# A gated recurrence and a low-rank mixer on one core: every operation in another order, the unread products placed anew

## The chip, the core and the metric

The kernel runs on one core of a Trainium2 chip. The core's engines work side by side, each through its own queue in the order in which the program issued to it: TensorE (PE in the profile, with PEld for its weight loads), VectorE (DVE), ScalarE (ACT), GpSimd (POOL) and SyncE (SP), which here issues nearly all DMA transfers. An instruction that needs another engine's result waits on a semaphore, and everything behind it in its queue waits with it. The metric is device time in microseconds (us), lower is better; the median of the kernel before is 626.9 us over 3 runs (626.64 to 627.37).

## What is computed

Two blocks in a row. The first is a recurrence over 768 steps for 4 batches, 8 heads of width 48; the second takes its output as a matrix of 4 x 768 x 384 and applies a rank-32 mixing along the sequence and a two-layer product along the channels:

```python
mag = np.sqrt(a_re * a_re + a_im * a_im)
scale = np.minimum(mag, 0.999) / (mag + 1e-06)
a_re_n, a_im_n = (a_re * scale, a_im * scale)
for t in range(S):
    new_re = ar * S_re - ai * S_im
    new_im = ar * S_im + ai * S_re
    S_re, S_im = (new_re + kv, new_im)
    y[:, :, t] = np.einsum('bhd,bhde->bhe', q[:, :, t], S_re)
...
h = xt @ U @ V
u = x + h.transpose(0, 2, 1)
ch = np.maximum(u @ w_ch1, 0.0) @ w_ch2
return (u + ch)
```

All inputs reach the kernel as float32 except the weights U, V, w_ch1 and w_ch2, whose 64-bit words the kernel converts itself.

## The kernel before

**Tiling.** The sequence is cut into 24 chunks of 128 steps (4 batches of 6), and two chunks make a group, so there are 12 groups. For each group, `gates` turns a_re and a_im into decays: ACT and DVE compute log magnitudes (tile GL, or GS as two halves), PE sums them within a chunk (tiles `es ps`, `ef ps`, and `tot` for blocks), ACT takes exponentials (es, ef, E), and SP moves E into T. The angles go the same way through `ph`, F and the sines in cs. `prep` multiplies q and k by these (DVE, tile qk and then QKC), and PE turns the result (tile `tr`), which ACT copies to QK. `chain` is then PE's own part of a chunk: `inner`, `corners`, `dk` and `y`, with DVE and ACT work between them. `mixer` runs over two chunks at a time, and only once a batch's 6 chunks are there: `rank`, `mixed`, `uTp`, then the large products `up` or `few` (w_ch1) and `down` (w_ch2). The weights are converted piece by piece on DVE and ACT in between (tags w1 and w2, tile stage).

**Order.** None of these functions issues anything. Each calls `plan.add` with an engine, a tag such as ("gates", 4) and a function that will issue the instructions. There are 2671 such operations. The table ORDER at the head of the file gives each its place, a number from 0 to 2670, under its engine and tag, and `Plan.order` sorts by it. The order on each engine's queue, and on SP's, is the order of these places; it also fixes the order in which buffers are handed out. The operations, their sizes and their costs do not depend on it.

**Unread products.** A second table, SPARE, maps a place to a number of units. Before the operation at that place, the program calls `idle` until those units are used up, at most 3 units (AHEAD) at a time. `idle(k)` issues one PE product of the 128 x 128 identity with k times 128 columns, into a PSUM tile that some later operation will overwrite from the start; nobody reads it. It finds no tile when every such tile is in use, and then issues nothing and the units are gone.

```python
            out += [-1] * SPARE.get(at[n], 0) + [n]
...
        while run:
            idle(min(run, AHEAD))
            run -= min(run, AHEAD)
```

Each 32-bit PE product leaves two MATMUL records in the trace, so 3 units are two records of 128 x 384. In the file before, these products are at L1519; the change shortens the file by one line, so that every line of the kernel stands one lower there (L1518).

Of the kernel before, what the change touches and what calls it, by code (L numbers as in the profile page):

```python
# [39 lines left out]
        ("POOL", "load"): {0: [14], 1: [34], 1.5: [84], 2: [31]},  # L40
        ("DVE", "load"): {1: [58]},
# [6 lines left out]
        ("ACT", "gates"): {0: [1, 2, 4, 6, 7, 16, 17, 22, 23, 29, 28, 45, 70, 71], 1: [24, 27, 38, 39, 41, 42, 46, 47, 65, 64, 67, 68], 2: [129, 108,  # L48
# [10 lines left out]
        ("DVE", "gates"): {0: [5, 8, 13, 18, 19, 54, 49], 1: [30, 21, 40, 43, 44, 51, 50], 2: [111, 143, 156, 185, 169], 4: [277, 322, 323, 372, 356],  # L59
# [10 lines left out]
        ("ACT", "angles"): {0: [72, 86, 98, 100, 103], 1: [76, 106, 112, 114, 126], 2: [210, 231, 251, 240, 241, 242, 263, 269, 271], 4: [375, 395,  # L70
# [5 lines left out]
        ("DVE", "angles"): {0: [81, 89], 1: [87, 107], 2: [211, 232, 252], 4: [376, 402, 425], 6: [589, 597, 602, 612, 625, 626, 665], 8: [698, 716,  # L76
# [4 lines left out]
        ("DVE", "prep"): {0: [85, 104, 110], 1: [121, 128, 145], 2: [226, 250, 265], 3: [203, 304, 309], 4: [373, 424, 427], 5: [443, 470, 472], 6:  # L81
# [99 lines left out]
class Plan:  # L181
# [33 lines left out]
    def order(self):  # L215
# [9 lines left out]
        for n in sorted(range(len(at)), key=lambda n: at[n]):  # L225
# [9 lines left out]
            done.add(n)  # L235
            out += [-1] * SPARE.get(at[n], 0) + [n]
        return out
# [1351 lines left out]
```

## Time and profile before

| | |
|---|---|
| median of 3 runs | 626.9 us |
| the profiled execution's own span | 627.0 us |
| PE busy with products | 609.9 us (97%) |
| PE busy with weight loads | 526.2 us (84%) |
| DVE busy | 499.7 us (80%) |
| ACT busy | 415.8 us (66%) |
| POOL busy | 38.1 us (6%) |
| DMA | 45.74 MB, mean 73 GB/s |

How to read it: a busy share is the part of the span in which an engine had work under way. It is an average over stages. The records of matmuls carry modelled ends, so that one product's end can lie after the next one's start; where a cost is wanted, the distance from one start to the next is the safer number. A timeline row gives start, duration, engine, line, operation and tiles, then how many records it merges, and in brackets how long the engine had been idle before and what it was waiting for. A row of the windows view gives, for a stretch of the span, how long each engine was busy in it, the clock that was granted to PE as a share of full speed, and the DMA share and rate.

### The profile page before, as it was taken

Reading aid. Unit: us, or ns where it says so; the run is one execution under the profiler, and the core shown is the slowest. Engines: PE = TensorE matmul, PEld = TensorE weight load, DVE = VectorE, ACT = ScalarE, POOL = GpSimd, SP = SyncE. Lnnn points to the kernel's source line nnn. Section 1 sums busy time; section 2 is a strip of 40 time slices with the busy share of each in tenths; the row PEclk is TensorE's granted clock in tenths of the full one; section 3 lists DMA queues with packets and bytes.
Section 4 is the critical chain, followed back from the end, with each engine's and each line's share of the span. In section 5 each row is a group of like instructions: output and inputs, shape, how many; then the busy total and the mean of one; then the engine's idle time right before and its main releaser. Section 6 shows DMA issues by size and latency. Waiting matters only on the chain.

```text
span 627.0 us, 23447 instructions
## 1 busy us (share of the span) xinstructions
PE 609.9 (97%) x10380; PEld 526.2 (84%) x10380; DVE 499.7 (80%) x887; ACT 415.8 (66%) x807; POOL 38.1 (6%) x79
## 2 busy tenths in 40 slices
PE   6998989999999999999999999999999999999998
PEld 3566767666889889889989989888999998999997
DVE  6899999888999979758977867788989884464554
ACT  6999999999898988687787867688433431202010
POOL 5000000000001010010000100000100100000100
PEclk7999999999999999999999999999999999999999
DMA  8864565644143252541512512601203020000101
GB/s 211 191 146 115 135 136 132 155 111 104 33 80 76 50 120 44 99 89 28 99 37 46 113 40 46 124 19 25 63 21 60 9 51 3 1 1 1 45 14 44
DMA packets 173685, 45.74 MB, mean 73 GB/s; under 512 B 167632, under 2 KB 170384, under 8 KB 173584
## 3 DMA queue, kind: packets, MB, share of 16 engines
q1 hardware_dynamic: 171376, 39.90, 30.1%
q0 software_dynamic: 2208, 4.35, 2.1%
q8 instruction: 81, 1.33, 0.9%
q14 instruction: 20, 0.16, 0.1%
HBM read 33.59 MB, written 4.72 MB: 61 GB/s over the span
## 4 chain that ended last, share of the span: by engine, by line
PE 77%; ACT 4%; DVE 3%; DMA 1%; issue 1%; SPq 0%; ACTq 0%; DVEq 0%
PE down L1356 24%; PE up L1122 15%; PE few L1222 11%; PE dk L996 3%; PE tr L860 3%; PE y L1035 3%; PE inner L910 2%; PE down L1313 2%; PE inner L907 2%; PE tot L741 2%; PE y L1027 2%; PE mixed L1089 2%; PE es ps L692 1%; PE ef ps L692 1%; PE uTp L1107 1%; PE corners L971 1%
## 5 line engine op out<-in xcount | busy, mean ns | idle before, releaser
L1122 PE MATMUL up<-uT,w 128*128 128x256 f32 x504 | 116.9, 383 | 0.0
L387 DVE TENSOR_TENSOR QK<-QK,T 112x512 f32<-112x512 f32 (+2 forms) x144 | 102.1, 732 | 8.4 <-PE inner L910 4.3
L1122 PEld LDWEIGHTS up<-uT,w 128*128 128x128 f32 x504 | 93.6, 190 | 12.5
L1356 PE MATMUL down<-w,h 128*128 128x192 f32 x396 | 72.2, 331 | 0.0
L384 ACT ACTIVATE gate<-gate 128x768 f32<-128x768 f32 (+1 forms) x82 | 64.8, 795 | 7.4 <-DVE GS L791 3.2
L1356 PEld LDWEIGHTS down<-w,h 128*128 128x128 f32 x396 | 64.1, 190 | 1.5 <-issue 0.7
L871 ACT COPY QK<-tr 112x512 f32<-112x512 f32 x96 | 51.2, 590 | 14.6 <-PE tr L860 14.3
L390 DVE TENSOR_TENSOR xo<-down,xo 128x192 f32<-128x192 f32 (+1 forms) x79 | 29.9, 387 | 27.5 <-PE down L1356 27.0
L387 DVE TENSOR_TENSOR QKC<-qk,cs 128x768 f32<-128x768 f32 x44 | 41.7, 955 | 6.3 <-ACT cs L384 3.6
L1230 ACT COPY h<-few 128x512 f32<-128x512 f32 x30 | 17.2, 586 | 40.8 <-PE few L1222 40.8
L1356 PE MATMUL down<-stage 128*128 128x192 f32 x198 | 37.6, 331 | 0.0
L1111 ACT COPY uT<-uTp 128x384 f32<-128x384 f32 x22 | 10.0, 479 | 41.4 <-PE uTp L1107 26.9
L1222 PE MATMUL few<-gate,w 128*128 128x128 f32 x280 | 34.8, 275 | 0.0
L1298 POOL DMA_DIRECT2D out_dram<-xo x32 | 19.2, 644 | 243.3 <-DVE xo L390 140.0
L860 PEld LDWEIGHTS tr<-ident,QKC 64*112 64x112 f32 x768 | 24.5, 130 | 10.7 <-issue 4.7
L1222 PEld LDWEIGHTS few<-gate,w 128*128 128x128 f32 x280 | 33.3, 192 | 0.0
L1356 PEld LDWEIGHTS down<-stage 128*128 128x128 f32 x198 | 32.1, 190 | 0.7 <-issue 0.2
L779 POOL DMA_DIRECT2D gate<-F x15 | 12.0, 799 | 327.9 <-DVE w L578 113.5
L860 PE MATMUL tr<-ident,QKC 64*112 64x64 f32 x768 | 29.4, 221 | 2.3 <-DVE QKC L387 1.6
L381 ACT ACT_TABLE_LOAD x24 | 30.8, 1283 | 1.1 <-PEq L1573 0.7
L384 ACT ACTIVATE h<-up 128x512 f32<-128x512 f32 x42 | 24.6, 596 | 9.8 <-PE up L1122 9.5
L976 ACT COPY AT<-corners 32x128 f32<-32x128 f32 x96 | 24.2, 255 | 9.6 <-PE corners L971 8.3
(200 smaller groups left out, 1285.4 us busy)
## 6 DMA issues: line engine op xcount, KB each, us to landing
stage<-in_moe_w_ch_dram SPq DMA_DIRECT2D x12, 768.0 KB, 5.0
qk<-in_q_dram SPq DMA_DIRECT2D x24, 192.0 KB, 3.2
qk<-in_k_dram SPq DMA_DIRECT2D x24, 192.0 KB, 2.7
VP<-in_v_dram SPq DMA_DIRECT2D x24, 192.0 KB, 3.6
gate<-in_a_re_dram SPq DMA_DIRECT2D x22, 192.0 KB, 3.4
gate<-in_a_im_dram SPq DMA_DIRECT2D x22, 192.0 KB, 3.4
AT<-DG SPq DMA_DIRECT2D x96, 32.0 KB, 2.3
T<-E SPq DMA_DIRECT2D x48, 48.0 KB, 2.9
```

What stands on the lines that cost most here:

```text
L381: ACT(1.37, rank, lambda: nc.scalar.preload_act_table_set(name), writes=[TABLE])
L384: return nc.scalar.activation(out=o, in_=i, func=f, **kw)
L387: nc.vector.tensor_tensor(out=o, in0=a, in1=b, op=OP.mult)
L390: nc.vector.tensor_tensor(out=o, in0=a, in1=b, op=OP.add)
L860: nc.tensor.transpose(out=get(*ps[r])[0:DQ, h], in_=get(*qkc)[at, h].rearrange("p u d -> p (u d)")[:, 0:DQ], identity=ident[at, at], tile_ ...
L871: nc.scalar.copy(out=to, in_=a)
L976: ACT(0.36, RR, lambda r=r, u=u: nc.scalar.copy(out=get(*ATi).rearrange("p (a u) t -> p a u t", u=2)[r:r + BLK, :, u, BLK:2 * BLK], in_=ge ...
L996: nc.tensor.matmul(out=get(*dk[r])[x:end, h], lhsT=get(*ks)[at, h, x // DP, 0:end - x], rhs=get(*VPi)[at, h], start=True, stop=True, tile_ ...
L1122: nc.tensor.matmul(out=get(*ps)[:, e], lhsT=w1[:, f, (ff + e) * 128:(ff + e + 1) * 128], rhs=get(*uT)[:, f], start=(f == 0), stop=(f == KD ...
L1222: nc.tensor.matmul(out=get(*ps)[:, q], lhsT=w()[:, q * 128:(q + 1) * 128], rhs=v[0](), start=(n == 0 and q == 0), stop=True, skip_group_ch ...
L1298: queue.dma_start(out=out[b, c * CH:(c + 1) * CH, lo:hi], in_=get("xo", i)[:, lo:hi])
L1356: nc.tensor.matmul(out=get(*to)[:, part], lhsT=x(j), rhs=y[:, j], start=(first and j == 0), stop=(j == KH - 1), skip_group_check=not first)
```

## The change

Both tables are replaced and nothing else: the same 2671 operations under the same engines and tags, with the same number under each, get other places, and SPARE asks for unread products at other places. Before, SPARE asked for 153 units at 41 places up to place 718. After, it asks for 229 units at 22 places up to place 619, 60 of them ahead of place 21. As the tables feed the same program, the built queues show what comes of it: before, 46 unread products of together 91 units stand on PE's queue, since `idle` found no tile for the rest; after, 83 products stand there, and they are all of the 229 units.

The first PE operations, `es ps` and `ef ps` of the first chunk, stand behind one product run of 8 units before and of 60 units after. The tables, cut to their beginnings (ORDER is some 140 lines):

```diff
 ORDER = {
-        ("SP", "load"): {0.0: [0, 3, 2666, 2654, 2670], 0.05: [11, 12], 0.1: [9], 1: [10], 1.2: [57], 1.3: [15, 59], 1.4: [83], 2: [35], 2.5: [56,
...
-        ("PE", "gates"): {0: [20, 32, 69], 1: [62, 63, 66], 2: [162, 163, 167, 168, 187, 188], 4: [331, 339, 343, 351, 352, 355], 6: [543, 525, 550,
...
+        ('SP', 'load'): {0.0: [1, 3, 2666, 2663, 2670], 0.05: [15, 6], 0.1: [8], 1: [27], 1.2: [22], 1.3: [73, 36], 1.4: [95], 2: [35], 2.5: [96, 66],
...
+        ('PE', 'gates'): {0: [21, 41, 52], 1: [45, 48, 54], 2: [156, 179, 161, 184, 185, 196], 4: [324, 344, 350, 355, 358, 360], 6: [532, 513, 533,
...
-SPARE = {20: 8, 32: 9, 62: 1, 66: 1, 73: 1, 82: 5, 91: 1, 113: 6, 116: 1, 119: 8, 140: 8, 153: 6, 157: 4, 167: 1, 168: 1, 207: 6, 216: 1, 217: 1, 282:
-         1, 352: 2, 436: 1, 514: 5, 518: 5, 527: 4, 546: 4, 547: 25, 551: 12, 596: 2, 601: 1, 606: 3, 624: 1, 632: 3, 646: 1, 653: 1, 664: 1, 672: 2,
-         678: 5, 694: 1, 695: 1, 717: 1, 718: 2}
+SPARE = {21: 60, 45: 13, 52: 3, 78: 13, 94: 6, 101: 21, 115: 9, 141: 28, 148: 6, 156: 4, 177: 8, 185: 3, 208: 5, 225: 4, 242: 2, 265: 13, 268: 4, 408:
+         9, 474: 4, 479: 3, 491: 6, 619: 5}
```

PE's queue in the order after, up to the first large block: 60 units, `es ps` and `ef ps` of chunk 0, 13 units, `es ps` and `ef ps` of chunk 1, 3 units, `tot`, two `ph` products, 13 units, two more `ph`, 6 units, the third kind of `ph`, 21 units, `tr` twice, 9 units, `dk`, `tr`, `inner`, 28 units. On SP's queue, the load of q for chunk 0 stands behind the first move of E into T; before, it stood ahead of all of them.

More of the change, by code (lines that the diff above doesn't have):

```diff
@@ L30 @@
 ORDER = {
[9 rows of a table removed]
-        ("POOL", "load"): {0: [14], 1: [34], 1.5: [84], 2: [31]},
-        ("DVE", "load"): {1: [58]},
[6 rows of a table removed]
-        ("ACT", "gates"): {0: [1, 2, 4, 6, 7, 16, 17, 22, 23, 29, 28, 45, 70, 71], 1: [24, 27, 38, 39, 41, 42, 46, 47, 65, 64, 67, 68], 2: [129, 108,
[10 rows of a table removed]
-        ("DVE", "gates"): {0: [5, 8, 13, 18, 19, 54, 49], 1: [30, 21, 40, 43, 44, 51, 50], 2: [111, 143, 156, 185, 169], 4: [277, 322, 323, 372, 356],
[10 rows of a table removed]
-        ("ACT", "angles"): {0: [72, 86, 98, 100, 103], 1: [76, 106, 112, 114, 126], 2: [210, 231, 251, 240, 241, 242, 263, 269, 271], 4: [375, 395,
[5 rows of a table removed]
@@ L76 @@
-        ("DVE", "angles"): {0: [81, 89], 1: [87, 107], 2: [211, 232, 252], 4: [376, 402, 425], 6: [589, 597, 602, 612, 625, 626, 665], 8: [698, 716,
[4 rows of a table removed]
-        ("DVE", "prep"): {0: [85, 104, 110], 1: [121, 128, 145], 2: [226, 250, 265], 3: [203, 304, 309], 4: [373, 424, 427], 5: [443, 470, 472], 6:
[6 rows of a table removed]
-        ("ACT", "prep"): {0: [115, 117, 120, 122], 1: [158, 147, 154, 160], 2: [266, 270, 283, 281], 3: [319, 320, 327, 318], 4: [442, 439, 446, 445],
[4 rows of a table removed]
-        ("DVE", "rest"): {0: [118, 149, 155, 175, 159, 170, 194], 1: [174, 229, 234, 259, 209, 235, 248, 253], 2: [288, 315, 325, 366, 291, 314, 324,
[8 rows of a table removed]
@@ L102 @@
-        ("DVE", "levels"): {0: [123, 135, 148, 136, 137, 152], 1: [177, 192, 202, 195, 198, 225], 2: [292, 302, 308, 301, 303, 312], 3: [328, 371,
[9 rows of a table removed]
-        ("ACT", "levels"): {0: [138], 1: [215], 2: [305], 3: [378], 4: [468], 5: [530], 6: [766], 7: [839], 8: [947], 9: [1006], 10: [1152], 11:
[14 rows of a table removed]
-        ("ACT", "rest"): {0: [191, 182, 200, 201, 219, 223, 222], 1: [255, 261, 256, 258, 280, 279, 278], 2: [342, 341, 336, 335, 385, 390, 391], 3:
[10 rows of a table removed]
-        ("ACT", "small"): {0: [595, 285, 307, 492, 396, 554, 590, 549, 623, 636], 1: [744, 791, 777, 807, 782, 856, 859], 2: [984, 978, 1088, 1139,
[4 rows of a table removed]
@@ L143 @@
-        ("DVE", "small"): {0: [246, 600, 631, 637, 640, 638, 685, 682, 603, 607, 731, 737], 1: [705, 741, 690, 817, 843, 844, 870, 871, 889, 913, 912,
[25 rows of a table removed]
-        ("POOL", "small"): {0: [932, 933], 1: [1119, 1116, 1117], 2: [1337, 1278, 1338], 3: [1670, 1446, 1515], 4: [1778, 1776, 1777], 5: [2049, 1855,
-        2008], 6: [2154, 2101, 2162], 7: [2343, 2276, 2342], 8: [2633, 2632, 2648], 9: [2629, 2634, 2663], 10: [2635, 2627, 2636]},
-        ("POOL", "angles"): {6: [615], 8: [708, 733], 10: [882, 931], 12: [1097], 14: [1273, 1302], 16: [1472, 1516], 18: [1669], 20: [1879, 1913],
@@ L172 @@
-        22: [2039, 2077]},
-        ("DVE", "mixing"): {7: [2018, 2019, 2021, 2030, 2032, 2024, 2040, 2102, 2108, 2115, 2120, 2125, 2027]},
-}
-SPARE = {20: 8, 32: 9, 62: 1, 66: 1, 73: 1, 82: 5, 91: 1, 113: 6, 116: 1, 119: 8, 140: 8, 153: 6, 157: 4, 167: 1, 168: 1, 207: 6, 216: 1, 217: 1, 282:
-         1, 352: 2, 436: 1, 514: 5, 518: 5, 527: 4, 546: 4, 547: 25, 551: 12, 596: 2, 601: 1, 606: 3, 624: 1, 632: 3, 646: 1, 653: 1, 664: 1, 672: 2,
-         678: 5, 694: 1, 695: 1, 717: 1, 718: 2}
[9 rows of a table added]
+        ('POOL', 'load'): {0: [9], 1: [51], 1.5: [597], 2: [39]},
@@ new lines @@
+        ('DVE', 'load'): {1: [26]},
[6 rows of a table added]
+        ('ACT', 'gates'): {0: [0, 2, 5, 11, 12, 14, 19, 24, 38, 34, 32, 42, 53, 57], 1: [17, 7, 28, 29, 31, 33, 43, 50, 47, 46, 49, 55], 2: [120, 82,
[10 rows of a table added]
+        ('DVE', 'gates'): {0: [10, 4, 13, 16, 20, 58, 25], 1: [18, 23, 30, 40, 44, 75, 64], 2: [126, 142, 149, 187, 166], 4: [275, 305, 323, 363,
[10 rows of a table added]
+        ('ACT', 'angles'): {0: [70, 83, 91, 86, 99], 1: [79, 97, 106, 107, 109], 2: [214, 231, 246, 245, 244, 249, 257, 259, 260], 4: [379, 406, 420,
[5 rows of a table added]
+        ('DVE', 'angles'): {0: [77, 84], 1: [80, 98], 2: [215, 232, 248], 4: [382, 407, 425], 6: [563, 579, 583, 600, 616, 617, 657], 8: [695, 713,
[4 rows of a table added]
@@ new lines @@
+        ('DVE', 'prep'): {0: [92, 100, 103], 1: [112, 116, 127], 2: [224, 262, 266], 3: [199, 300, 308], 4: [410, 418, 430], 5: [442, 459, 482], 6:
[6 rows of a table added]
+        ('ACT', 'prep'): {0: [111, 110, 114, 119], 1: [146, 133, 151, 155], 2: [267, 271, 273, 272], 3: [315, 322, 325, 326], 4: [443, 449, 451, 448],
[4 rows of a table added]
+        ('DVE', 'rest'): {0: [113, 147, 152, 181, 154, 171, 191], 1: [158, 217, 220, 241, 243, 258, 263, 269], 2: [289, 320, 335, 352, 318, 321, 331,
[8 rows of a table added]
+        ('DVE', 'levels'): {0: [123, 130, 138, 128, 132, 145], 1: [165, 183, 188, 190, 197, 229], 2: [283, 296, 306, 294, 301, 312], 3: [327, 342,
[9 rows of a table added]
@@ new lines @@
+        ('ACT', 'levels'): {0: [139], 1: [212], 2: [302], 3: [364], 4: [477], 5: [519], 6: [754], 7: [840], 8: [925], 9: [1032], 10: [1167], 11:
[14 rows of a table added]
+        ('ACT', 'rest'): {0: [182, 200, 178, 205, 227, 218, 233], 1: [252, 261, 237, 238, 284, 282, 285], 2: [368, 366, 372, 349, 400, 403, 402], 3:
[10 rows of a table added]
+        ('ACT', 'small'): {0: [596, 291, 394, 457, 330, 520, 609, 537, 625, 655], 1: [738, 798, 762, 788, 799, 834, 866], 2: [948, 987, 1121, 1147,
[4 rows of a table added]
+        ('DVE', 'small'): {0: [295, 606, 628, 631, 633, 663, 673, 680, 611, 613, 739, 744], 1: [692, 701, 691, 837, 833, 844, 885, 891, 926, 960, 981,
[25 rows of a table added]
@@ new lines @@
+        ('POOL', 'small'): {0: [997, 790], 1: [1114, 1151, 1155], 2: [1383, 1381, 1458], 3: [1545, 1465, 1522], 4: [1844, 1672, 1725], 5: [1920, 1966,
+        1975], 6: [2132, 2169, 2175], 7: [2299, 2379, 2380], 8: [2529, 2421, 2631], 9: [2556, 2554, 2559], 10: [2650, 2628, 2651]},
+        ('POOL', 'angles'): {6: [615], 8: [711, 746], 10: [879, 921], 12: [1093], 14: [1246, 1280], 16: [1435, 1479], 18: [1650], 20: [1853, 1885],
+        22: [2024, 2056]},
+        ('DVE', 'mixing'): {7: [2017, 2032, 2020, 2080, 2117, 2043, 2083, 2089, 2129, 2135, 2118, 2120, 2035]},
+}
```

244 rows, old and new, of the table ORDER are left out of this document.

## The prediction

> **What bounds the kernel now.** First the page's head: how long the span is, and how much of it PE works.
>
> ```profile
> span 627.0 us, 23447 instructions
> PE 609.9 (97%) x10380; PEld 526.2 (84%) x10380; DVE 499.7 (80%) x887; ACT 415.8 (66%) x807; POOL 38.1 (6%) x79
> ```
>
> PE is idle for 627.0 - 609.9 = 17.1 us in all. Where, and which engine sets the pace there, is read from the windows; the columns after the stretch are PE, PEld, DVE, ACT and POOL busy, then the granted clock.
>
> ```profile
> 0.00:10.00 10.00, 4.79 (x8) 2.69 (x9) 5.30 (x19) 5.96 (x11) 7.23 (x30) 0.90 0.78 184
> 10.00:20.00 10.00, 9.34 (x54) 5.69 (x53) 8.31 (x19) 7.25 (x16) 1.17 (x3) 0.75 1.00 240
> 20.00:50.00 30.00, 29.03 (x562) 19.07 (x560) 29.27 (x47) 29.37 (x55) 0.00 (x0) 1.00 0.67 155
> 50.00:110.00 60.00, 54.47 (x1435) 42.55 (x1434) 58.89 (x95) 57.35 (x113) 0.00 (x0) 1.00 0.55 130
> 110.00:160.00 50.00, 48.70 (x518) 32.00 (x518) 44.27 (x64) 45.40 (x77) 2.50 (x3) 1.00 0.48 116
> 160.00:500.00 340.00, 339.61 (x6454) 304.48 (x6453) 281.97 (x494) 249.35 (x494) 21.28 (x33) 1.00 0.31 61
> ```
>
> From 160 us on, PE is bound by its own work: 0.39 us idle in 340. Ahead of 160 three engines are nearly full at once (from 50 to 110, DVE 58.89 of 60), PE has its gaps there, and nearly all unread products stand there too. So the kernel is a PE queue that never catches up: whatever makes PE later in the first 160 us is carried to the end. The end itself is fixed too: after PE's last product only one addition and the last store follow.
>
> ```profile
> 622.83 1.14 PE L1356 MATMUL down<-w,more 128*128 128x192 f32 x6
> 624.01 0.36 DVE L390 TENSOR_TENSOR xo<-down,xo 128x192 f32<-128x192 f32 x1 [1.39 <-PE down L1356]
> ```
>
> The products end at 623.97, 3.0 us before the span does. The first product starts at 1.42 (below). Of the 17.1 idle, 1.4 lie ahead of everything, 3.0 behind it, and 17.1 - 1.4 - 3.0 = 12.7 between products.
>
> **The change part by part.** The operations are the same, so PE's real work stays, and the sum is over what stands between: unread products, the cold clock, and idle time.
>
> Unread products now. The groups of L1519:
>
> ```profile
> L1519 PE MATMUL tr<-ident 128*128 128x384 f32 (+2 forms) x34 | 13.3, 515 | 1.4 <-POOL ident masks.py:199 1.4
> L1519 PE MATMUL up<-ident 128*128 128x384 f32 (+2 forms) x38 | 11.4, 413 | 0.0
> L1519 PE MATMUL fix<-ident 128*128 128x128 f32 (+2 forms) x10 | 3.0, 379 | 0.0
> L1519 PE MATMUL down<-ident 128*128 128x384 f32 (+1 forms) x4 | 1.3, 406 | 0.0
> L1519 PE MATMUL ph<-ident 128*128 128x128 f32 (+1 forms) x4 | 1.1, 352 | 0.0
> L1519 PE MATMUL ef ps<-ident 128*128 128x128 f32 x2 | 0.5, 326 | 0.0
> ```
>
> That is 92 records, 46 products, 30.6 us busy. This counts modelled ends that overlap the next start, so I price them by starts, from the timeline of PE:
>
> ```profile
> 1.42 3.58 PE L1519 MATMUL tr<-ident 128*128 128x384 f32 x6 [1.42 <-POOL ident masks.py:199]
> 8.79 1.62 PE L696 MATMUL es ps<-GL,mid 128*128 128x384 f32 x2 [3.79 <-DVE GL L390]
> 10.21 4.05 PE L1519 MATMUL tr<-ident 128*128 128x384 f32 x6
> 14.05 1.25 PE L696 MATMUL ef ps<-GL,fore 128*128 128x384 f32 x2
> 15.13 0.39 PE L1519 MATMUL tr<-ident 128*128 128x128 f32 x2
> 15.35 0.81 PE L696 MATMUL es ps<-GL,mid 128*128 128x384 f32 x2
> 16.00 0.81 PE L696 MATMUL ef ps<-GL,fore 128*128 128x384 f32 x2
> ...
> 17.69 1.09 PE L735 MATMUL tot<-total,GL 128*64 128x32 f32 x32 [0.66 <-ACT es L384]
> ...
> 26.23 0.27 PE L860 MATMUL tr<-ident,QKC 64*112 64x64 f32 x1 [0.23 <-DVE QKC L387]
> ...
> 32.10 1.99 PE L1519 MATMUL up<-ident 128*128 128x384 f32 x6
> 34.02 0.66 PE L860 MATMUL tr<-ident,QKC 64*112 64x64 f32 x16
> ...
> 44.22 1.56 PE L1519 MATMUL up<-ident 128*128 128x384 f32 x4
> 45.70 0.68 PE L1027 MATMUL y<-VP,AT 64*64 64x48 f32 x32
> 46.92 0.49 PE L1519 MATMUL up<-ident 128*128 128x128 f32 x2
> 47.24 0.81 PE L799 MATMUL ph<-fourth,prefix 128*128 128x384 f32 x2
> ```
>
> The run of 8 units at 32.10 costs 1.92 to the next start, the run of 6 at 44.22 costs 1.48: 0.22 a unit, and 1.48 - 6 x 0.22 = 0.16 once per run. A lone unit costs 0.22 (15.13) to 0.32 (46.92), so the extra per run is 0.00 to 0.16; I take 0.12. The modelled ends overlap the next start by 0.07 (34.02) to 0.17 (15.35); with some 33 runs in the queue at about 0.12 that takes 4 us off the 30.6, so the unread products cost 26.7 us now.
>
> Unread products after: 229 units x 0.22 = 50.4, 22 runs x 0.12 = 2.6. The first 8 units ran cold at 1.42, 3.58 instead of 1.92, 1.7 more; the same 8 stand first in the new queue and pay that again. Together 54.7 us, 28.0 more than now.
>
> Cold clock. The first `es ps` and `ef ps` start 1.42 and 1.08 ahead of what follows (8.79, 14.05), the second ones 0.65 (15.35): being cold costs them 0.77 + 0.43 = 1.2 us. In the new order no gap stands ahead of them, so this goes: -1.2.
>
> The Trainium skill (TensorE: Matmul & The Clock Gate, Part 1) says that PE's clock is halved by default, is released after about 3.4 us of activity and falls back after an idle window as long. The trace agrees, with 0.90 and 0.75 granted in the first two stretches, the 3.79 us gap between cold runs, and 1.00 after. By this rule the new order is cold once, as the sum has it; without it, a second cold phase would keep the 1.2 and cost the 9 units at 10.21 about 1.9 more, 646 instead of 643.
>
> Idle time. The first data reach PE at 8.79. In the new order PE gets to `es ps` only after 60 units: 1.42 + 3.58 + 52 x 0.22 = 16.4, that is 7.6 us after the data could be there. From there to the first transposes (`tr`), the new queue holds 56 more units (12.3 us), four `es`/`ef` products and five `ph` products at 0.65 (5.9), `tot` (1.0) and some run extras (0.6): 36.2 us, where the timeline of before has 26.23. PE, which waited for DVE there, is now 10 us behind. So the gaps between products should close nearly everywhere, as from 160 to 500: I leave 2 of the 12.7 us for round trips such as the 0.66 ahead of `tot`, which the ACT's work between two products sets however late PE is. That is -10.7.
>
> What follows for the others: DVE and ACT are made to wait for PE in the first 30 us. DVE is busy for 5.30 + 8.31 + 29.27 + 58.89 = 101.8 of the first 110 us; with PE 10 to 16 us late the same work has that much more time. The moves on SP's queue cost nothing as long as they stay ahead of PE; the rival below has the one that may not.
>
> Sum: 627.0 + 28.0 - 1.2 - 10.7 = 643.1. The profiled execution's 627.0 and the median 626.9 agree, so the forecast is 643. Bounds: at best a unit costs 0.65 / 3 = 0.217, no run costs extra and no gap is left, 49.7 + 1.7 - 26.7 = 24.7, so 627.0 + 24.7 - 1.2 - 12.7 = 637.8. At worst every run costs 0.16 (55.6, 28.9 more) and all gaps stay: 654.7.
>
> **The rivals.** First, the gaps stay or others open: the longer wait ahead of PE is passed on to what feeds it. The place is SP's queue:
>
> ```profile
> qk<-in_q_dram SPq DMA_DIRECT2D x24, 192.0 KB, 3.2
> 4.17 4.06 SPq L539 DMA_DIRECT2D qk<-in_q_dram  x1
> 18.36 0.28 ACT L384 ACTIVATE E<-tot 112x128 f32<-112x128 f32 x1 [0.44 <-PE tot L735]
> 19.45 0.75 SPq L719 DMA_DIRECT2D T<-E  x1
> 20.24 0.58 SPq L539 DMA_DIRECT2D qk<-in_k_dram  x1
> 25.22 0.96 DVE L387 TENSOR_TENSOR QKC<-qk,cs 128x768 f32<-128x768 f32 x1 [0.17 <-ACT cs L384]
> ```
>
> Now q of chunk 0 is issued at 4.17, long ahead of T<-E. After, it is issued behind it, and T<-E waits for `tot`, which stands behind 89 units: about 23.8 to its end, 0.44 and two exponentials of 0.28 on ACT, 0.75 for the move, 0.58 for the issue, 3.2 to land, so 29.3, then two DVE passes of 0.96 (qk, QKC): transposes at 31.2 at the earliest. PE comes there at 36.2 and has 5 us to spare. If `tot` or the queue slips by more, and with it the weight loads behind them, PE waits again; with the 12.7 us of idle unchanged the time is 627.0 + 28.0 - 1.2 = 654. For it: the whole first stage is a chain of such round trips. Against it: PE's 10 us of lag.
>
> Second, part of the added products is free: in the first 160 us PE's busy time may hide waits behind modelled ends, and products would fill these. With 4 to 8 us of that the time is 635 to 639. For it: PE is called full from 20 to 50 while DVE and ACT are full too. Against it is one kind of product over the whole kernel:
>
> ```profile
> L860 PE MATMUL tr<-ident,QKC 64*112 64x64 f32 x768 | 29.4, 221 | 2.3 <-DVE QKC L387 1.6 <-DVE F L807 0.6
> ```
>
> Its 48 lots of 16 take 29.4 / 48 = 0.61 on average, the early one at 34.02 takes 0.66: hardly anything is hidden in it. The Trainium skill (Perfetto Trace Analysis, Identifying the Most-Contended Engine) says that PE's matmul busy share is a poor measure of how much room it has, and that its weight loads' share is better. By that, with 84%, the added products would find room and the time would stay near 626, for which I leave the 0.01 of no change: the stretch from 160 to 500, gapless with 304.48 of 340 us in weight loads, shows no such room.
>
> Third, the other side: PE does not set the first stage, DVE does, and the new order feeds DVE sooner. DVE is idle 20 - 5.30 - 8.31 = 6.4 us in the first 20 us; if the order brings 4 of that forward and every product stands in time that PE would have waited anyway, the result is 623. It decides from the point where the first transposes start at 26 or sooner; but 116 units stand ahead of them, 25.5 us with nothing else done, so PE would have to drop them.
>
> Fourth, the change does not do what it says: before, only 91 of the 153 units asked for found a tile. Were it the same share after, 136 units would cost 29.9 + 2.6 + 1.7 = 34.2, 7.5 more than now, and with the gaps as they are the time would be 633. But the built queue has all 83 products, so it gets no chance.
>
> **How the numbers follow.** The forecast (637.8 to 648) has 0.72, the stalls that stay (648 to 656) 0.20, partly free products (630 to 638) 0.05, the other side 0.02, no change 0.01. The range for 8 times in 10 takes the forecast's own range and half of the stalls: 638 to 652. A measurement of this kernel tells 0.2%, about 1.3 us, from no change; so faster 0.02, same 0.01, slower 0.97.
>
> **What would show it.** Right: 166 records of unread products, the first 60 units of them in one block from 1.42 to about 16; `es ps` at about 16, the first `tr` at about 36; the clock at 1.00 from about 5 us on; PE's idle time down from 17.1 to 5 to 9 us; from 160 us on no gaps, so that everything runs some 16 us later than now. Wrong: the first `tr` well before 33, or PE idle for 12 us and more between products, with DMA or SP-fed loads as the releaser, or real products that take another time in other neighbourhoods, which I priced at nothing.

## The result and the profile after

The changed kernel takes 670.33 us (median of 4 runs, 667.28 to 672.54), the kernel before in the same series 627.13 (626.64 to 628.0): 1.067 times as long, with a 95% interval of 1.0622 to 1.0717. The time rose by 43.2 us, where the prediction had 16.1. The profiled execution took 667.28 and was the fastest of the four. One of the four executions of a kernel further down (the new order with the first block alone, 658.05 us at a clock of 0.971) was in a slower state and is left out of that kernel's figures.

The head of the page after, and the windows in the stretches used for before (PE, PEld, DVE, ACT and POOL busy, the granted clock, the DMA share and rate):

```profile
span 665.5 us, 23611 instructions
PE 640.8 (96%) x10454; PEld 543.6 (82%) x10454; DVE 498.1 (75%) x887; ACT 414.7 (62%) x807; POOL 37.6 (6%) x79
```

```profile
0.00:10.00 10.00, 8.58 (x22) 5.08 (x23) 5.75 (x23) 6.87 (x13) 7.03 (x30) 1.00 0.83 223
10.00:20.00 10.00, 10.00 (x34) 5.92 (x32) 3.68 (x9) 2.62 (x7) 0.82 (x4) 1.00 0.56 128
20.00:50.00 30.00, 30.00 (x365) 19.05 (x364) 21.27 (x35) 20.92 (x37) 0.00 (x0) 1.00 0.34 83
50.00:110.00 60.00, 58.96 (x1214) 42.11 (x1214) 54.36 (x85) 53.42 (x104) 0.00 (x0) 1.00 0.66 156
110.00:160.00 50.00, 47.08 (x808) 32.52 (x804) 42.93 (x68) 46.29 (x85) 0.96 (x1) 1.00 0.47 114
160.00:500.00 340.00, 326.47 (x5992) 287.27 (x5992) 269.33 (x461) 250.67 (x486) 22.33 (x34) 1.00 0.32 64
```

The first 160 us look as forecast: PE is full from 1.4 to 50 us, DVE and ACT, nearly full there before, have room, and the granted clock reads 1.00 in every stretch. What was not forecast stands in the last row: between 160 and 500 us PE is idle for 13.53 us, where before it was idle for 0.39.

Every microsecond of PE's span belongs to one of four things: unread products, real products (each counted up to the next start), idle time between products, and what lies ahead of the first and behind the last. Summed over all records of the two profiled executions:

| us | before | after | rise | predicted |
|---|---|---|---|---|
| unread products | 26.8 | 53.4 | +26.6 | +28.0 |
| real products | 583.1 | 587.3 | +4.2 | -1.2 |
| idle between products, up to 160 us | 12.3 | 4.0 | -8.3 | -10.7, both rows together |
| idle between products, from 160 us on | 0.4 | 16.3 | +15.9 | |
| ahead of all and behind all | 4.4 | 4.4 | 0.0 | 0.0 |
| sum | 627.0 | 665.4 | +38.4 | +16.1 |

The table accounts for 38.4 of the 43.2. The profiled execution is 3.1 us below the median of the changed kernel, and its time is 1.8 us longer than its span, while the prediction took the 627.0 us span of before for its time.

The first rows of PE's timeline after carry the early steps (start, duration, engine, line, tiles, records merged, idle before):

```profile
1.42 14.65 PE L1518 MATMUL tr<-ident 128*128 128x384 f32 x40 [1.42 <-POOL ident masks.py:199]
15.91 0.81 PE L695 MATMUL es ps<-GL,mid 128*128 128x384 f32 x2
...
30.50 4.68 PE L1518 MATMUL tr<-ident 128*128 128x384 f32 x14
35.11 1.11 PE L859 MATMUL tr<-ident,QKC 64*112 64x64 f32 x32
```

`es ps` starts at 15.91 (forecast 16.4), the first `tr` at 35.11 (forecast 36.2), and none of these rows has idle time in brackets after the first.

The late idle time is no single wait. The costliest waits of PE after, and one of ACT's waits before and after (who waited for what, us in total, times, longest):

```profile
PE y L1034 <- ACT xo L1045: 3.0, 9, 0.6
PE tr L859 <- ACT AT L975: 2.0, 1, 2.0
PE inner L906 <- DVE DG L921: 1.8, 2, 0.9
...
PE up L1121 <- ACT h L383: 1.4, 1, 1.4
PE down L1355 <- DVE more L1347: 1.3, 1, 1.3
```

```profile
ACT GS L788 <- DMA gate<-F: 1.3, 2, 0.8
```

```profile
ACT GS L787 <- DMA gate<-F: 12.2, 8, 3.0
```

The last two rows are before and after. In the angle path POOL adds the last row of one chunk's F to the next chunk's `gate` by a 1.5 KB transfer, and ACT copies the result to GS. In the new order ACT often reaches that copy before the row has landed. One such place, in ACT's and in PE's timeline after:

```profile
203.54 0.26 ACT L975 COPY AT<-corners 32x128 f32<-32x128 f32 x1
206.31 0.51 ACT L787 CAST GS<-gate 128x384 fp32r<-128x384 f32 x1 [2.51 <-DMA gate<-F]
206.84 0.26 ACT L975 COPY AT<-corners 32x128 f32<-32x128 f32 x1
```

```profile
204.49 0.71 PE L859 MATMUL tr<-ident,QKC 64*112 64x64 f32 x17
207.16 0.66 PE L859 MATMUL tr<-ident,QKC 64*112 64x64 f32 x15 [1.95 <-ACT AT L975]
```

ACT stands 2.51 us at the GS copy. The AT copy behind it needs nothing that is missing, but it is behind in the queue, and PE's transposes wait 1.95 us for it. The list of waits names "ACT AT" for PE; the cause is two queues away. Here the row took 4.6 us to land, against 2.5 at the median, and in the other two of the three longest such waits 3.9 and 3.7; no run shows why these landed late.

### The profile page after: what moved, and what is told of

Its sections match the earlier page's. It is cut to its first block, busy times and chain, and to the rows that moved or that the text cites. A ratio compares the mean times of both kernels' runs of the same rounds, so it can differ in the third digit from the quotient of the medians.

```text
span 665.5 us, 23611 instructions
## 1 busy us (share of the span) xinstructions
PE 640.8 (96%) x10454; PEld 543.6 (82%) x10454; DVE 498.1 (75%) x887; ACT 414.7 (62%) x807; POOL 37.6 (6%) x79
## 4 chain that ended last, share of the span: by engine, by line
PE 68%; issue 13%; ACT 9%; DMA 5%; DVE 3%; POOL 1%; SPq 0%; DVEq 0%; POOLq 0%; ACTq 0%
PE down L1355 19%; PE few L1221 10%; PE up L1121 9%; PE tr L1518 5%; DMA gate<-F 3%; PE up L1518 3%; PE tr L859 3%; ACT gate L383 2%; PE dk L995 2%; PE inner L909 2%; PE y L1034 2%; PE down L1312 2%; PE tot L740 1%; PE inner L906 1%; ACT L380 1%
## 5 line engine op out<-in xcount | busy, mean ns | idle before, releaser
L1229 ACT COPY h<-few 128x512 f32<-128x512 f32 x30 | 17.4, 586 | 55.9 <-PE few L1221 53.8
L389 DVE TENSOR_TENSOR xo<-down,xo 128x192 f32<-128x192 f32 (+1 forms) x79 | 30.1, 386 | 23.8 <-PE down L1355 23.6
L921 DVE COPY_PREDICATED DG<-mask,inner 128x128 f32<-128x128 int32 (+1 forms) x72 | 24.2, 343 | 16.4 <-PE inner L906 13.4
L1518 PE MATMUL tr<-ident 128*128 128x384 f32 (+1 forms) x90 | 31.1, 495 | 1.4 <-POOL ident masks.py:199 1.4
L1233 DVE CUSTOM_DVE_ANT_1 h<-few,h 128x512 f32<-128x512 f32 x30 | 20.1, 688 | 14.5 <-PE few L1221 14.0
```

Of the source, the lines that this page charges most:

```text
L389: nc.vector.tensor_tensor(out=o, in0=a, in1=b, op=OP.add)
L921: nc.vector.copy_predicated(out=to, mask=part(mask[:, n], "p").unsqueeze(1).to_broadcast(list(to.shape)), data=a if t == BLK else a.rearra ...
L1518: nc.tensor.matmul(out=to[:, 0:k * 128].rearrange("p (k m) -> p k m", k=k), lhsT=ident, rhs=ident.unsqueeze(1).to_broadcast([128, k, 128]) ...
```

## The experiments

Each time is a median, and each rise is against the kernel before in the same series (its medians were 628.58, 628.35, 628.65, 628.27 and 629.39). Nine of the eighteen medians lie outside every range that was expected for them: the old order without unread products, the new head, the stalled products, both shorter blocks, the first block alone in the new order, the copies put in between, and the row transfer left out of the new tail and of the whole change. The unread products and the two halves of the order were first taken apart.

**No unread products**, in the new and in the old order:

```diff
-SPARE = {21: 60, 45: 13, 52: 3, 78: 13, 94: 6, 101: 21, 115: 9, 141: 28, 148: 6, 156: 4, 177: 8, 185: 3, 208: 5, 225: 4, 242: 2, 265: 13, 268: 4, 408:
...
+SPARE = {}
```

> The changed kernel's order with no unread product at all (SPARE empty); everything else as in it. Its 83 unread products took 53.4 us from start to start, and PE has 17.6 us of gaps after 160 us. Theory A (the later gaps are made by the order itself: producers and consumers stand closer together on the queues): the products fall away, most of that time comes back as waiting for DVE and ACT in the first 150 us as the old order had it, and the gaps after the first stage stay at 13 us or more; 645 to 660 us. Theory B (the later gaps are the echo of a first stage that the unread products made 15 us late): gaps after the first stage fall under 5 us, 625 to 640 us. Theory C (unread products cost nothing, they only stand where PE waits): no change within 1%, 662 to 674 us.

> The kernel before, with no unread product (SPARE empty). They take 26.7 us of PE there. If they stand in time that PE waits for others anyway, and hold the clock up, taking them away leaves the time at 627 to 632 us with 35 us or more idle in the first 160 us, and a granted clock that falls more often. If they are on the path, the time falls to 605 to 620 us.

The new order takes 652.0 (650.35 to 656.67, rise 23.4), the old one 633.65 (630.87 to 638.21, rise 5.1). So the order costs 18.3 us with no unread product in either. In the old order these products are worth 5.1 us to the kernel; in the new one they cost 43.2 - 23.4 = 19.8. The granted clock of the runs without them was 0.97 to 0.99 in both orders. At the same clock of 0.989 a run of the new order took 650.35 and one of the old 632.13, so the difference of 18 us is not the clock's.

**One half of the order each.** The head is the 750 operations that stand first in the old order, the tail is the rest. In the first kernel the head is sorted as in the new order, with its unread products, and the tail keeps the old order; in the second it is the other way round. The tables against the after and the before:

```diff
-        ('SP', 'load'): {0.0: [1, 3, 2666, 2663, 2670],
+        ('SP', 'load'): {0.0: [1, 3, 2666, 2654, 2670],
...
-        ('SP', 'load'): {0.0: [0, 3, 2666, 2654, 2670],
+        ('SP', 'load'): {0.0: [0, 3, 2666, 2663, 2670],
```

> The first 750 operations of the kernel before (its first 156 us) in the changed kernel's order among each other, with the changed kernel's 229 units at the same operations; from there on the order of before. Theory A: the head costs what the trace of the changed kernel shows ahead of 160 us (26.7 us more of unread products, 8.3 us less of gaps, 1.2 less of cold clock: 14 to 18 us) and the tail has no gaps of its own: 640 to 646 us. Theory B: the tail gets gaps of 10 us and more although its order is the old one: 652 us and more.

> The first 750 operations as before, in the order of before and with its unread products; all others in the changed kernel's order. Theory A: the head costs nothing, the tail has 14 to 18 us of gaps after 160 us: 641 to 650 us. Theory B: no late head, so no gaps: 625 to 632 us.

The new head takes 651.64 (651.21 to 653.84, rise 23.1), the new tail 641.87 (641.15 to 645.01, rise 13.3); together 36.4 of the 43.2. The windows from 160 to 500 us, of the new head with the old tail, then of the old head with the new tail:

```profile
160.00:500.00 340.00, 337.50 (x6286) 297.80 (x6285) 282.23 (x485) 258.28 (x501) 22.28 (x34) 1.00 0.33 66
```

```profile
160.00:500.00 340.00, 329.56 (x6177) 294.13 (x6178) 270.21 (x473) 241.62 (x478) 20.21 (x31) 1.00 0.31 61
```

2.50 us idle against 10.44: the late gaps come with the tail's own order, also with nothing changed ahead of it. The new head costs more than was expected for it, although its tail stays nearly gapless.

**Moving copies away from the places that stall.** First in the new order, seven copies of y that stand between the two writers of one y tile (L1026 and L1034) go behind the second writer; then 19 PE operations that wait are moved 1 to 3 places later besides. One chunk of each:

```diff
-        ('PE', 'rest'): {11: [1251, 1254, 1261, 1264, 1268],
+        ('PE', 'rest'): {11: [1251, 1254, 1261, 1264, 1267],
-        ('ACT', 'rest'): {11: [1212, 1252, 1242, 1210, 1269, 1266, 1270],
+        ('ACT', 'rest'): {11: [1212, 1252, 1242, 1210, 1269, 1268, 1270],
...
-        ('PE', 'prep'): {8: [889, 894],
+        ('PE', 'prep'): {8: [889, 903],
```

> The changed kernel with one thing undone: in chunks 0, 5, 11, 15, 19, 21 and 23 its order puts ScalarE's copy of one half of tile y between PE's two writers of that tile (before(0) or inside, and before(1)); the old order has the copy behind both in every chunk. Here the seven copies stand right behind the second writer, all else as in the changed kernel. If the second writer waits for that copy (9 waits of y for ACT xo, 3.0 us in the trace, and 2.5 us more inside these products than before), the time falls by 2 to 5 us against the changed kernel, to 663 to 668 us at a median of 670. If the copies are only where the profile puts the blame, and PE is held by something else at these places, it stays within 1 us.

> As the run before, and besides 19 PE operations that waited 0.25 to 1.95 us after 100 us (12.9 us together) each stand one to three PE operations later in PE's queue, so that 0.4 to 4 us of other products come before them. Theory A (the order itself leaves too little between producer and consumer): the gaps close and PE idles 5 to 8 us after 100 us instead of 19; 652 to 659 us. Theory B (PE has to wait in the tail because DVE, ACT or loads arrive late as such): the waits move to the next operation in the queue, the time stays within 3 us of the run before.

The copies: 667.33 (664.49 to 672.04), whose range overlaps that of the changed kernel. The stalled products as well: 680.81 (680.19 to 684.06), 13.5 us worse, and still 8 us at the same granted clock of 0.985 (680.19 against 672.04). The wait list of the latter starts with others:

```profile
PE dk L996 <- ACT xo L1044: 4.4, 1, 4.4
PE down L1356 <- DVE xo L390: 3.0, 4, 1.7
```

The waits moved and grew: PE's idle time from 160 us on is 20.0, against 14.6 with the copies alone. That a product which gives way makes its own consumers late in turn would explain this; no run shows it by itself.

**A shorter first block**, in the whole change and, later, with the old tail:

```diff
-SPARE = {21: 60, 45: 13, 52: 3, 78: 13, 94: 6, 101: 21, 115: 9, 141: 28, 148: 6, 156: 4, 177: 8, 185: 3, 208: 5, 225: 4, 242: 2, 265: 13, 268: 4, 408:
+SPARE = {21: 24, 45: 13, 52: 3, 78: 13, 94: 6, 101: 21, 115: 9, 141: 28, 148: 6, 156: 4, 177: 8, 185: 3, 208: 5, 225: 4, 242: 2, 265: 13, 268: 4, 408:
```

> The changed kernel with the first block of unread products cut from 60 units to 24; they then end at about 8.5 us, close to the 9.15 us at which the first data reach PE without any. If lateness at the start is carried to the end, as the prediction has it: 36 units of 0.215 us less, 7 to 8 us, 661 to 664 us. If the head is bound by the chain through DVE, ACT and SP instead, the time stays above 667 us.

> New head with a first block of 24 units in place of 60, all other unread products as in the changed kernel, old tail. If lateness from the first block is carried to the end one to one: 651.6 less 7.7, 643 to 645 us. If it grows on its way, as the 14 us in the whole kernel say: 636 to 641 us.

36 units are 36 x 0.215 = 7.7 us (a unit is a third of the 0.64 from `es ps` to `ef ps`). Removing them takes the whole change to 655.87 (654.71 to 657.66), a rise of 27.5 instead of 43.2, so they are worth 15.7. With the old tail they are worth no more than their own length: 646.74 (643.96 to 649.73), a rise of 17.4 instead of 23.1, 5.7. At a granted clock of 0.997 or more the runs with the old tail are 6.9 apart (651.34 and 651.21 against 643.96 and 644.83) and those of the whole change 12.0 (667.28 and 668.39 against 655.87 at the median). In the profile of the whole change with the shorter block, idle time from 160 us on is 10.6 instead of 16.3:

```profile
160.00:500.00 340.00, 330.75 (x6172) 293.48 (x6172) 271.81 (x471) 249.58 (x486) 21.61 (x33) 1.00 0.32 64
```

So the lag of the 60 units costs more with the new tail than with the old one. With 24 units head and tail cost together less than the sum of their own rises (27.5 against 17.4 + 13.3), with 60 more (43.2 against 36.4). Why the lag makes the tail's waits longer isn't settled.

**The old order with the new order's SP and POOL queues:**

```diff
-        ("SP", "load"): {0.0: [0, 3, 2666, 2654, 2670], 0.05: [11, 12], 0.1: [9], 1: [10],
+        ('SP', 'load'): {0.0: [0, 3, 2666, 2650, 2670], 0.05: [11, 9], 0.1: [10], 1: [30],
```

> The kernel before, with SyncE's and GpSimd's queues (loads, moves, stores, the additions into F's rows) in the changed kernel's order; PE, DVE and ACT queues are the old ones, unread products too. If the order of the transfers has no part in the loss: 626 to 631 us. If loads that now stand behind PE-dependent moves (q of chunk 0 behind T<-E) hold up the head, as the prediction's first rival has it: 632 us and more, with DMA as the releaser in the first 60 us.

689.84 (687.53 to 693.0), a rise of 61.5, and PE's costliest wait is

```profile
PE y L1029 <- DMA AT<-DG: 25.8, 9, 6.8
```

The transfers of one order don't fit the computing of the other. Only 2.1 of the 25.8 us lie in the first 60 us, where the wait was expected. This shows what a misfit on that queue costs, not that the new order has one; there `AT<-DG` is waited for twice, 0.9 us in all.

**The first block alone**, 24 units in the old order with all else kept, and 24 units as the only unread products of the new one:

```diff
-SPARE = {20: 8, 32: 9,
+SPARE = {20: 24, 32: 9,
...
-SPARE = {21: 60, 45: 13, 52: 3, 78: 13, 94: 6, 101: 21, 115: 9, 141: 28, 148: 6, 156: 4, 177: 8, 185: 3, 208: 5, 225: 4, 242: 2, 265: 13, 268: 4, 408:
...
+SPARE = {21: 24}
```

> The kernel before with its first block of unread products at 24 units instead of 8, so that PE works without a gap from 1.42 us to about 8.5 us, where the first data come; all else as before. If the second cold phase (0.77 + 0.43 us in es and ef, some 1.9 us in the 9 units at 10.21) lies on the path: 1 to 3 us less, 625 to 627.5 us at a median of 628.5 before. If other engines set the pace there: within 0.8 us of before. If the units make the first es late: 630 us and more.

> The changed kernel with a first block of 24 units and none of the other 169 (36 us of PE). The run with a first block of 24 and all others took 655.9 us, the one with none at all 652.0 us with its clock falling to 0.77 from 20 to 50 us. If the other units lie mostly where PE would wait, and only keep the clock up: 650 to 657 us. If they delay the first stage as the first block did (14 us for 36 units): 638 to 647 us.

The first takes 627.1 over 12 runs (625.75 to 630.06) against 628.65, 0.9975 times as long with an interval of 0.9962 to 0.9989: the one version that beats both kernels. Its PE timeline:

```profile
1.42 7.83 PE L1521 MATMUL tr<-ident 128*128 128x384 f32 x16 [1.42 <-POOL ident masks.py:199]
9.09 0.81 PE L698 MATMUL es ps<-GL,mid 128*128 128x384 f32 x2
9.73 2.10 PE L1521 MATMUL tr<-ident 128*128 128x384 f32 x6
11.67 0.81 PE L698 MATMUL ef ps<-GL,fore 128*128 128x384 f32 x2
```

The block ends 0.3 us after the data could be there (8.79 in the trace of before), no cold stretch follows (the 9 units take 2.10 instead of 4.05), and `ef ps` starts at 11.67 instead of 14.05. The second kernel takes 649.12 (646.45 to 649.92), a rise of 20.5 instead of the 23.4 without any. With the other 169 units behind its block it took 655.87, a rise of 27.5: these units are 36 us long and cost 7.0, for without them PE waits more and its clock falls (0.98 over the run against 1.00).

**Copies between the two writers of y.** The mechanism of the 3.0 us in PE's wait list is tried both ways: the new tail with its five such copies put behind the second writer, and the old order with ten put in between. One chunk of each:

```diff
-        ('PE', 'rest'): {15: [1674, 1668, 1706, 1707, 1709],
+        ('PE', 'rest'): {15: [1674, 1668, 1706, 1707, 1708],
-        ('ACT', 'rest'): {15: [1692, 1658, 1662, 1686, 1711, 1708, 1710],
+        ('ACT', 'rest'): {15: [1692, 1658, 1662, 1686, 1711, 1709, 1710],
...
-        ("PE", "rest"): {6: [813, 745, 742, 854, 855],
+        ('PE', 'rest'): {6: [813, 745, 742, 854, 856],
-        ("ACT", "rest"): {6: [834, 832, 837, 838, 865, 862, 869],
+        ('ACT', 'rest'): {6: [834, 832, 837, 838, 865, 855, 869],
```

> The old head with the new tail (641.9 us), and in it ScalarE's copy between the two writers of y moved behind the second writer in chunks 11, 15, 19, 21 and 23. If that wait is real and costs 0.3 us visibly and as much again inside the product: 1.5 to 3.5 us less, 638.5 to 640.5 us. If not: 641 to 643 us.

> The reverse on the kernel before: in the ten chunks where nothing else stands in the way (0, 5, 6, 9, 12, 14, 15, 17, 18, 19) ScalarE's copy of the first half of y is put just ahead of PE's second writer of that tile; PE's, DVE's, SP's and GpSimd's queues stay as they were. If the second writer waits for the copy: 10 times 0.3 to 0.6 us, 631 to 635 us at 628.5 before, with as many waits of y for ACT xo. If not: within 1 us of before.

The new tail: 642.12 (639.8 to 642.63), a rise of 13.5 against 13.3, so nothing came back. The old order: 637.08 (636.64 to 639.21), a rise of 8.4 or 0.84 us for each of the ten. Its group of second writers and its wait:

```profile
L1037 PE MATMUL y<-GM,QK 112*64 112x48 f32 x384 | 19.0, 227 | 4.0 <-ACT xo L1048 3.3 <-DVE QK L389 0.7
```

```profile
PE y L1037 <- ACT xo L1048: 3.3, 10, 0.9
```

The mechanism is real: a copy that reads one half of y makes the writer of the other half wait, and with it PE's whole queue. But in the new tail taking it away gave nothing back. That PE then waits for something else there is likely; no run shows it.

**The row transfer of F.** The 15 transfers of POOL are left out, in the new tail with its copies behind, in the old order as a control, and in the whole change:

```diff
-                POOL(0.8, R2, lambda: nc.gpsimd.dma_start(out=of(z, i)[0:1], in_=fo(i - 1)[CH - 1:CH], accum_op=OP.add),
+                POOL(0.8, R2, lambda: None,
```

> The old head with the new tail and the copies of y behind both writers (642.1 us), and in it the 15 transfers gate<-F on GpSimd's queue left out: the last row of a chunk's F is no longer added to the first row of the next chunk's angles, so the phase isn't carried from chunk to chunk in batches 2 to 4. If ScalarE's waits for these transfers make the tail's loss: 630 to 636 us. If the tail is slow for other reasons: 639 to 643 us.

> The control: the kernel before with the same 15 transfers left out. ScalarE waits 1.3 us for them there, so 626 to 629 us, within 1.5 us of before. If the transfers cost by other ways (DMA, GpSimd), it falls further.

> The changed kernel with the same 15 transfers left out. ScalarE waits 12.2 us for them there. If they make the tail's part of the loss: 655 to 662 us at a median of 670. If not: 667 us and more.

The new tail falls to 638.08 (636.79 to 638.93), a rise of 9.8 instead of 13.5. The control stays at 628.82 (627.12 to 630.83), 1.0008 times before, interval 0.9992 to 1.0024. The whole change falls to 665.87 (660.89 to 669.36), a rise of 37.6 instead of 43.2, with runs that spread over 8.5 us; at a granted clock of 1.00 it took 660.89, where the changed kernel took 667.28 and 668.39. So some 4 us of the tail are this wait, which costs nothing in the old order. PE's wait of 2.0 us for ACT's AT copy, still there with the copies behind,

```profile
PE tr L861 <- ACT AT L977: 2.0, 1, 2.0
```

is gone from the list when the transfer is left out, as the cause named above would have it. In the new tail without it PE still has 6.02 us idle from 160 to 500:

```profile
160.00:500.00 340.00, 333.98 (x6359) 298.54 (x6360) 274.61 (x483) 242.99 (x484) 9.65 (x18) 1.00 0.31 61
```

**ACT's GS copies 1 to 8 operations later** in the new tail with its copies behind, so that the row has landed when ACT comes to them:

```diff
-        ('ACT', 'angles'): {14: [1208, 1241, 1259, 1276, 1288,
+        ('ACT', 'angles'): {14: [1208, 1241, 1267, 1276, 1297,
```

> The old head with the new tail and the copies of y behind both writers (642.1 us), and in ten chunks ScalarE's copy of the angles into GS, which waits for the transfer gate<-F, one to eight ScalarE operations later, as far as the order of buffers lets it; nothing is left out. ScalarE's work between F and that copy grows from 2.4 us on average to about 3.3. If the distance is what counts: ScalarE waits 5 to 8 us instead of 10, and 636 to 641 us. If it makes other things late: 642 us and more.

646.34 (643.78 to 647.59), a rise of 18.1 instead of 13.5, although ACT's wait fell from 10.3 to

```profile
ACT GS L789 <- DMA gate<-F: 4.3, 3, 2.2
```

That what hangs on GS came late in its turn is the likely reason; no run shows it.

**The new head's order alone**: the new head with the old tail, and no unread products.

```diff
-SPARE = {21: 60, 45: 13, 52: 3, 78: 13, 94: 6, 101: 21, 115: 9, 141: 28, 148: 6, 156: 4, 177: 8, 185: 3, 208: 5, 225: 4, 242: 2, 265: 13, 268: 4, 408:
...
+SPARE = {}
```

> New head (first 750 operations) with no unread product, old tail. If head and tail add up, 652.0 less the tail's 13.3: 637 to 641 us, some 5 us of it from the colder clock, as the old order has without its unread products (633.7 against 628.6). If the head's order costs nothing by itself: 632 to 635 us.

640.9 (634.53 to 643.36), a rise of 11.5. Against the 5.1 of the old order without unread products the head's order costs 6.4, and its unread products 23.1 - 6.4 = 16.7: the 11.6 that they add here and the 5.1 that those of before were worth.

## Why the prediction was wrong

The forecast of 643.1 is 27.2 us below the 670.33. By the traces, the idle time is 18.3 of these, real products are 5.4 and unread products -1.4; the other 4.9 are the distance of the median from the profiled span.

The 43.2 us, by the runs: unread products 16.7 (the new head against its order alone), the head's order 6.4, the tail's order 13.3, and 6.8 that arise only when both come together. The first two are rough, since the runs of the head's order alone spread over 8.8 us. That the 16.7 lies next to the prediction's sum of 16.1 is partly luck: in the trace of the new head with the old tail, unread products take 27.9 more, as forecast, but the idle time falls by 5.2 instead of 10.7. Neither half of the order was given a price of its own.

**Unread products: right.** 83 products in 166 records, 53.4 us against 54.7, and +26.6 against +28.0. The block of 60 units and the starts of `es ps` and `tr` came within 1.1 us. (The prediction puts `tot` behind 89 units; by the queue it lists they are 76, and its 23.8 for the end of `tot` fits 76; the trace has 23.1.) Each product took its full length on PE, so the second rival falls. The Trainium skill (Perfetto Trace Analysis, Identifying the Most-Contended Engine) takes the weight loads' share as a better measure of room than the matmul share. By it the time would have stayed near 626, and it did not. What the products cost the kernel is less than their length, though, as without them PE waits and its clock falls: 19.8 us for all 83 in the new order.

**Cold clock: right.** The first 60 units take 14.49 us to the start of `es ps`, 1.6 more than 60 x 0.215: PE starts cold, for which the forecast had 1.7, though the window's row reads 1.00. No second cold stretch follows. The twelve `es ps` and twelve `ef ps` records of this line took 4.2 + 3.8 + 1.8 + 1.6 = 11.4 us before; the groups after:

```profile
L695 PE MATMUL ef ps<-GL,fore 128*128 128x384 f32 x8 | 3.4, 512 | 0.0
L695 PE MATMUL es ps<-GL,mid 128*128 128x384 f32 x8 | 3.2, 486 | 0.0
L695 PE MATMUL ef ps<-w,fore 128*128 128x384 f32 x4 | 1.6, 512 | 0.0
L695 PE MATMUL es ps<-w,mid 128*128 128x384 f32 x4 | 1.5, 486 | 0.0
```

Their busy time adds up to 9.7; with overlapping ends cut at the next start, 9.72 before became 8.50 after, which is the 1.2 forecast. The Trainium skill (TensorE: Matmul & The Clock Gate, Part 1) has the clock fall back after an idle window of about 3.4 us. The trace agrees: once PE has started its longest wait is 2.0 us, and the clock stays at 1.00.

**Idle time: wrong, and this is the step that failed.** It read: "So the gaps between products should close nearly everywhere, as from 160 to 500: I leave 2 of the 12.7 us". Ahead of 160 us they did, 12.3 to 4.0. But the gapless stretch from 160 to 500 was taken as a property of a PE that is behind, and it was a property of the old order: with the old head and only the tail's order changed, 10.44 us of gaps open there. One place shows how. For the twelve chunks with a row transfer in the tail, the ACT work that stands between the last write that the transfer needs (F of the chunk before, or ACT's own angles) and the GS copy is 2.2 us instead of 3.4 on average (the order's distances, with durations from the trace). From the start of its issue the row takes 2.0 us at the median to land before and 2.5 after, so ACT stops and holds back its queue. The idle time between products, forecast to fall by 10.7, rose by 7.6: the late part rose by 15.9, and the step was off by 18.3.

**Real products: priced at nothing, took 4.2 more**, 5.4 without the cold clock's part. The second writers of y account for 2.9 of it; the group of before stands first, those of after behind it:

```profile
L1035 PE MATMUL y<-GM,QK 112*64 112x48 f32 x384 | 15.9, 225 | 0.7 <-DVE QK L387 0.7
L1035 PE MATMUL y<-G,QK 112*64 112x48 f32 x320 | 12.9, 223 | 0.0
```

```profile
L1034 PE MATMUL y<-GM,QK 112*64 112x48 f32 x384 | 18.0, 226 | 2.4 <-ACT xo L1045 2.4
L1034 PE MATMUL y<-G,QK 112*64 112x48 f32 x320 | 13.7, 225 | 0.6 <-ACT xo L1045 0.6
```

The mean of one product hardly changes (225 to 226 ns), but the group is busy for longer, so its products overlap less: part of a wait shows there and not as idle time. The prediction named this as a way in which it could be wrong and gave it no price.

**The rivals.** The first, stalls that stay or open, is what happened, with 654 for the time and a wrong place: q of chunk 0 behind the move of E held nothing up, since PE has no idle time from 20 to 50. The stalls opened after 160 us, where it had not looked. The third falls with the first `tr` at 35.11, the fourth with the 166 records.

**What stays open.** Of the tail's 13.3 us, some 4 are ACT's wait for the row. The rest is spread over waits of 0.2 to 1.3 us (in the trace without the row transfer) and 2.9 us of longer real products, and moving single waits away gave nothing back that the ranges can tell, or made it worse, in all four kernels that did so. No run shares it out among them, and none shows how the head's lag makes it grow by 6.8. Part of the spread between runs comes with the clock: the changed kernel's four runs had 1.0 and 1.0 (667.28, 668.39), 0.99 and 0.989 (672.26, 672.54).

## What to carry to other kernels

A stretch without gaps tells of the order that was profiled, not of the engine: when an order is replaced as a whole, compare for each wait, on every queue, how much work stands between producer and consumer in both orders, and give the new order a price of its own before summing what else changes. Ask of products that only keep the clock up where they stand: here 24 units instead of 8, ending as the first data come, gained 1.6 us in the old order, 36 more behind them cost between 5.7 and 15.7, and 169 spread over the rest of the head cost 7.0 of their 36 us. In the four kernels that moved what waits or what it waits for, nothing was gained that the ranges can tell: see first who needs the result of what you move.

## What the runs showed that was not expected

- A copy that reads one half of a PSUM tile between the two groups of products that write its halves cost 0.84 us each in the old order, 0.33 of it as idle time of PE in front (4.0 against 0.7 for ten) and 0.31 as longer products (19.0 against 15.9); the rest is not located.
- 36 unread units too many, 7.7 us of PE time, cost 5.7 us with the old tail and 15.7 with the new one.
- The old computing order with the new order's transfers is 61.5 us slower, more than the whole new order (43.2).
- Without unread products the old order's granted clock was 0.98 to 0.99 over the run, and the kernel 5.1 us slower, though PE had 91 units less to do.
